# Turning q before its feature map, finer Sinkhorn tasks, and a second engine for one scaling: a change to a fused linear-attention and Sinkhorn mixture-of-experts kernel

## The chip, the cores and the metric

One core of one Trainium2 chip. The metric is the time of one execution on the device, in microseconds (us); lower is better. "Faster" and "slower" mean by over 2%. The profile's span is some 1.8 us shorter than the time of the same run.

The engines: TensorE (PE in the profile), VectorE (DVE), ScalarE (ACT), GpSimd (POOL). PSUM is the memory that TensorE writes; SBUF is the on-chip memory for everything else. "Turned" means transposed; a "cast" copies to another number format; an "eviction" copies a result out of PSUM, so that the PSUM bank can be filled again. kv, den, num and xt are TensorE's steps of attention, and kvz, qpT, rden, xn and xT are what the other engines make around them.

## The reference, cut to what matters

```python
def phi(x):                                   # feature map
    return np.where(x > 0, x, np.exp(x) - 1.0) + 1.0      # = max(x + 1, min(exp(x), 1))
q_p, k_p = phi(q), phi(k)                     # q, k, v: (8, 8, 576, 64) float32
kv = einsum('bhsd,bhse->bhde', k_p, v);  z = k_p.sum(axis=2)
x  = (q_p @ kv) / (q_p . z + 1e-6)            # -> x: (4608, 512)

P = exp(x @ w_gate - max)                     # (4608, 8)
for _ in range(8):                            # Sinkhorn: rows, then columns
    P /= P.sum(1) + 1e-9;  P /= P.sum(0) + 1e-9;  P *= N / E
for e in range(8):
    out += P[:, e:e+1] * (relu(x @ w1[e]) @ w2[e])
```

Attention is small; the eight experts are nearly all of TensorE's work. Expert 0 is computed beside attention, to fill TensorE's waits, and is scaled by its column of P once Sinkhorn is done.

## The kernel before

The kernel does not issue instructions in the order of its text. It describes tasks (engine or choice of engines, estimated us, dependencies, buffers), and a planner written in Python simulates them with these estimates and emits each engine's instruction list in the order in which the simulated tasks start. So an estimate changes the order of instructions and the choice of engine, not only a number in a table.

```python
class _Plan:
    def add(self, eng, fn, deps=(), prio=0.0, acq=(), use=(), lat=0.0, after=0.0): ...
    #  eng: ("dve", 0.49) or a choice {"dve": 0.6, "act": 1.17};  acq: takes a buffer of a pool
    def run(self):
        while left:
            ...                                   # the task that can start first, by prio
            t["start"] = te;  t["on"] = e;  t["done"] = te + t["eng"][e] + t["lat"]
            free[e] = te + max(0.0, t["eng"][e] - self.OVER.get(e, 0.0))
```

One attention block (two pairs of heads of one batch element; 16 blocks, n = 0 to 15). q and k take the same path: Exp on ScalarE, min and max on VectorE, all from SBUF. Then phi(q) is turned on TensorE, and copied out of PSUM:

```python
for nm in "kq":
    def f_e(_, ...):
        nc.scalar.activation(out=ge["tile"], in_=gin[nm]["tile"], func=AF.Exp)            # L266
    def f_t(e, ...):
        if e == "act":
            nc.scalar.add(out=..., in_=gin[nm]["tile"], add=1.0)                            # L272
    def f_m(_, ...):
        nc.vector.tensor_scalar(out=e, in0=e, scalar1=1.0, op0=ALU.min)                     # L275
        if g_["on"] == "act":
            nc.vector.tensor_tensor(out=o, in0=o, in1=e, op=ALU.max)                        # L278
        else:
            for r in range(2):
                nc.vector.scalar_tensor_tensor(out=o[:, r], in0=gin[nm]["tile"][:, r], scalar=1.0,
                                               in1=e[:, r], op0=ALU.add, op1=ALU.max)       # L281
... v is cast to float16 on GpSimd:  fadd(("pool", 1.3), f_v, ...)                          # L225
... kv_ps (banks ye2, ye3) <- tk, vv  (f_kv, L306);  kvz <- kv_ps
for j0, j1 in ((0, 5), (5, NJ)):
    gp = S_.grp(p_att)                                    # one of two "att" banks of PSUM
    def f_qt(...): nc.tensor.transpose(qt_ps, tq[:, j], ident)                              # L332
    def f_qc(e, ...): copy(e, qpT, qt_ps)                 # ScalarE or VectorE
... den (L347), rden, num (L371), xn = num * rden, xt (transpose, L387), xT <- xt
```

Expert 0: layer 1 writes `hq` in two PSUM banks (L536), its relu `h` is on ScalarE (L540), layer 2 writes `ye` (L706), then come its copy to `acc` and the scaling by P:

```python
def f_s(_, tt=tt, gg=gg):
    nc.vector.tensor_scalar(out=acc[g][:, tt, :], in0=acc[g][:, tt, :], scalar1=P_sb[:, gg, 0:1], op0=ALU.mult)
tf = add({"act": 0.59, "dve": 0.69}, f_fin, ...)
tf = add(("dve", 0.49), f_s, deps=[tf, p_done], prio=NG + g - 400.0)
```

The softmax here doesn't subtract the row's maximum and nothing guards it: scores larger than these inputs give would overflow.

Of the kernel before, what the change touches and what calls it, by code (L numbers as in the profile page):

```python
# [17 lines left out]
class _Plan:  # L18
# [13 lines left out]

    def add(self, eng, fn, deps=(), prio=0.0, acq=(), use=(), lat=0.0, after=0.0):

        if isinstance(eng, tuple):
            eng = {eng[0]: eng[1]}
        k = len(self.t)
        t = {"eng": eng, "fn": fn, "prio": prio, "acq": tuple(acq), "lat": lat, "kids": [], "nd": 0,
             "ready": after, "done": None, "id": k}
        self.t.append(t)  # L40
        for d in set(x for x in deps if x is not None):
            self.t[d]["kids"].append(k)
            t["nd"] += 1
        for g in list(acq) + list(use):
            g["users"].append(k)
        return k
# [5 lines left out]
    def run(self):  # L52
# [26 lines left out]
        while left:  # L79
# [25 lines left out]
            t["done"] = te + t["eng"][e] + t["lat"]  # L105
            free[e] = te + max(0.0, t["eng"][e] - self.OVER.get(e, 0.0))
            end = max(end, t["done"])
            for g in t["acq"]:
# [14 lines left out]
def kernel(  # L123
# [57 lines left out]
    p_in = {n: S_.pool(2) for n in "kvq"}  # L181
    p_e = S_.pool(2)
    p_t = {n: S_.pool(2) for n in "kq"}
# [8 lines left out]
    def load_w(ten, nm, pl, ap, cut, e, prio, parts=1, after=0.0, deps=()):  # L192
# [6 lines left out]
        for i in range(parts):  # L199
            def fn(_, i=i):  # L200
                dst, a, off = g["tile"], [list(x) for x in ap], e * DM * F
                if parts > 1:
                    n = a[cut][1] // parts
                    off += i * n * a[cut][0]
                    a[cut][1] = n
                    dst = dst[:, i * n:(i + 1) * n, :] if cut == 1 else dst[:, :, i * n:(i + 1) * n]
                nc.gpsimd.dma_start(out=dst, in_=AP(tensor=ten.tensor, offset=off, ap=a))
            ti = add(("pool", 1.0), fn, use=[g], prio=prio, deps=[tal])
            ts_.append(add(("dma", 6.0 / parts), lambda _: None, deps=[ti], use=[g], prio=prio, lat=2.6))
            w_last[0] = ti  # L210
# [15 lines left out]

    w_last, in_prev = [None], [None]
    front_ids = []
    xt_done = {}
# [7 lines left out]
    def att(b, g):  # L237
# [3 lines left out]
        def ps_home(i):  # L241
            if n < 2 and i < 2:
                return p_ye[i], yps, f"ye{i}"
            return p_att, aps, "att"

        src = [[NJ * D, P], [2 * S * D, 2], [1, NJ * D]]
        gin, tin, gt, tph = {}, {}, {}, {}
        for nm, ten in (("k", k), ("q", q), ("v", v)):
            gr = gin[nm] = S_.grp(p_in[nm])

            def fn(_, gr=gr, nm=nm, ten=ten):
                gr["tile"] = fp.tile([P, 2, NJ, D], FP32, tag=nm + "in", name=nm + "in", bufs=2)
                (nc.gpsimd if n in (2, 3) else nc.sync).dma_start(
                    out=gr["tile"].rearrange("p r j d -> p r (j d)"),
                    in_=AP(tensor=ten.tensor, offset=(b * H + 4 * g) * S * D, ap=src))
            ti = fadd(("pool", 1.0) if n in (2, 3) else ("sp", 0.45), fn, acq=[gr], prio=pr,
                      deps=[w_last[0] if n in (2, 3, 4) else None, in_prev[0]])
            in_prev[0] = ti
            tin[nm] = fadd(("dma", 1.55), lambda _: None, deps=[ti], use=[gr], prio=pr, lat=2.6)
        for nm in "kq":  # L260
            ge = S_.grp(p_e)
            gt[nm] = S_.grp(p_t[nm])

            def f_e(_, ge=ge, nm=nm):
                ge["tile"] = fp.tile([P, 2, NJ, D], FP16, tag="e", name="e" + nm)
                nc.scalar.activation(out=ge["tile"], in_=gin[nm]["tile"], func=AF.Exp)  # L266

            def f_t(e, g_=gt[nm], nm=nm):
                g_["tile"] = fp.tile([P, NJ, 2, D], FP16, tag="t" + nm, name="t" + nm)
                g_["on"] = e  # L270
                if e == "act":
                    nc.scalar.add(out=g_["tile"].rearrange("p j r d -> p r j d"), in_=gin[nm]["tile"], add=1.0)  # L272

            def f_m(_, ge=ge, g_=gt[nm], nm=nm):
                nc.vector.tensor_scalar(out=ge["tile"], in0=ge["tile"], scalar1=1.0, scalar2=None, op0=ALU.min)  # L275
                o = g_["tile"].rearrange("p j r d -> p r j d")
                if g_["on"] == "act":
                    nc.vector.tensor_tensor(out=o, in0=o, in1=ge["tile"], op=ALU.max)  # L278
                else:
                    for r in range(2):  # L280
                        nc.vector.scalar_tensor_tensor(out=o[:, r], in0=gin[nm]["tile"][:, r], scalar=1.0,  # L281
                                                       in1=ge["tile"][:, r], op0=ALU.add, op1=ALU.max)
            te = fadd(("act", 1.17), f_e, deps=[tin[nm]], acq=[ge], use=[gin[nm]], prio=pr)
            tt_ = fadd({"dve": 0.6, "act": 1.17}, f_t, deps=[tin[nm]],
                       acq=[gt[nm]], use=[gin[nm]], prio=pr)
            tph[nm] = fadd(("dve", 1.35), f_m, deps=[te, tt_], use=[ge, gt[nm], gin[nm]], prio=pr)
        gvv = S_.grp(p_vv)
# [5 lines left out]
        def f_v(e):  # L293
            copy(e, gvv["tile"][:, :, :, 0:D], gin["v"]["tile"])
        tvv.append(fadd(("pool", 1.3), f_v, deps=[ta, tin["v"]],
                        use=[gvv, gin["v"]], prio=pr))
        vcast[n] = tvv[0]
# [24 lines left out]
        def f_qa(_):  # L322
            gq["tile"] = fp.tile([P, 2, NJ, PW], FP16, tag="qpT", name="qpT")
        tqa = fadd(("none", 0.0), f_qa, deps=[tph["q"]], acq=[gq], prio=pr)
        tq = []
        for j0, j1 in ((0, 5), (5, NJ)):
            gp = S_.grp(p_att)

            def f_qt(_, j0=j0, j1=j1, gp=gp):
                gp["tile"] = aps.tile([P, 5, 2, PW], FP16, tag="att", name="qt_ps")  # L330
                for j in range(j0, j1):
                    nc.tensor.transpose(gp["tile"][:, j - j0, :, :].rearrange("p h w -> p (h w)"),  # L332
                                        gt["q"]["tile"][:, j, :, :].rearrange("p r d -> p (r d)"), ident)

            def f_qc(e, j0=j0, j1=j1, gp=gp):
                copy(e, gq["tile"][:, :, j0:j1, :].rearrange("p h j w -> p j h w"), gp["tile"][:, 0:j1 - j0])
            t1 = fadd(("pe", 0.06 * (j1 - j0)), f_qt, deps=[tph["q"], tqa], acq=[gp], use=[gt["q"]], prio=pr)
            tq.append(fadd({"act": 0.12 + 0.1 * (j1 - j0), "dve": 0.17 + 0.057 * (j1 - j0)}, f_qc, deps=[t1, tqa],
                           use=[gp, gq], prio=pr))
        js = [0, 2, 4, 6, 7]  # L340
# [74 lines left out]
    def sinkhorn():  # L415
# [9 lines left out]
        for it in range(8):  # L425
            def f_a(_, it=it):
                if it == 0:
                    nc.vector.tensor_reduce(ut, P0_sb, AXX.X, ALU.add)
                    nc.vector.tensor_scalar(out=Qr, in0=ut, scalar1=EPS, scalar2=None, op0=ALU.add)
                else:  # L430
                    nc.vector.tensor_tensor(out=wt, in0=P0_sb, in1=cc[:, None, :].broadcast_to([P, NTT, E]),
                                            op=ALU.mult)
                    nc.vector.tensor_reduce(ut, wt, AXX.X, ALU.add)
                    nc.vector.scalar_tensor_tensor(out=Qr, in0=Qr, scalar=EPS, in1=ut, op0=ALU.mult, op1=ALU.add)
                nc.vector.reciprocal(Rr, Qr)
                nc.vector.tensor_tensor(out=wt, in0=P0_sb, in1=Rr[:, :, None].broadcast_to([P, NTT, E]),
                                        op=ALU.mult)
                nc.vector.tensor_reduce(gs, wt.rearrange("p g e -> p e g"), AXX.X, ALU.add)
            gc = S_.grp(p_att)
# [5 lines left out]
            def f_d(_, it=it, gc=gc):  # L445
# [7 lines left out]
                nc.vector.reciprocal(cc, Dc)  # L453
            a = add(("dve", 2.85), f_a, deps=last, prio=-200.0)
            c = add(("pe", 0.2), f_c, deps=[a], acq=[gc], prio=-200.0, lat=0.15)
            last = [add(("dve", 0.65), f_d, deps=[c], use=[gc], prio=-200.0)]
# [238 lines left out]
    def unit_plain(e, g, gW=None, tW=None):  # L695
# [15 lines left out]
        for tt in range(4):  # L711
# [9 lines left out]

            def f_s(_, tt=tt, gg=gg):
                nc.vector.tensor_scalar(out=acc[g][:, tt, :], in0=acc[g][:, tt, :],
                                        scalar1=P_sb[:, gg, 0:1], scalar2=None, op0=ALU.mult)
            if e == 0:
                tf = add({"act": 0.59, "dve": 0.69}, f_fin, deps=[ty[tt], t_close if g >= NA else None],
                         use=[gy[tt]], prio=g - 400.0)
                tf = add(("dve", 0.49), f_s, deps=[tf, p_done], prio=NG + g - 400.0)
                for dh in range(2):
# [195 lines left out]
```

## Time and profile before

| | before |
|---|---|
| median, 3 runs | 982.81 us (982.53 to 983.16) |
| profiled run | 983.97 us, span 982.2 |
| TensorE busy | 962.2 us, 98% |
| TensorE idle before 125 us, 125 to 950 us, after | 14.1, 0.08, 5.8 us |

The profile's lines are in the prediction below. How to read them: a page line gives busy time and share of each engine; the 40 digits are the busy share of equal slices in tenths; a window row gives a stretch, then the busy us of PE, PEld, DVE, ACT and POOL, then clock and DMA; a gap line gives the start and length of a group of TensorE instructions, with the idle time before it and the instruction that ended it in brackets; a group line ends with count, total busy us, mean ns of one, and the idle time before it.

### The profile page before, as it was taken

How to read it: one execution, taken by the hardware profiler on the slowest of the kernel's cores; microseconds unless marked ns; L12 is line 12 of the kernel's file. 1: busy time of each engine (PE TensorE's matmuls, PEld its weight loads, DVE VectorE, ACT ScalarE, POOL GpSimd, SP SyncE). 2: the span in 40 equal slices, each digit the busy share in tenths (PEclk: the TensorE clock that was granted, in tenths of full speed). 3: DMA queues.
4: the chain of work that ended last, by engine and by line, in shares of the span. 5: the costliest groups of instructions: out<-in, count | busy, mean ns of one | idle time of the engine just before them, and what ended most of it. 6: DMA issues, size and time to landing. Idle time of an engine off the chain costs nothing.

```text
span 982.2 us, 21403 instructions
## 1 busy us (share of the span) xinstructions
PE 962.2 (98%) x8716; PEld 792.7 (81%) x8716; DVE 771.7 (79%) x1561; ACT 563.2 (57%) x1034; POOL 127.9 (13%) x171
## 2 busy tenths in 40 slices
PE   7899999999999999999999999999999999999997
PEld 4455564488888888888888888888888888888885
DVE  6898869967777777777777777777777777777774
ACT  4798754565555555555555555555555555555552
POOL 4111200001111111111111111111111111111110
PEclk9999999999999999999999999999999999999999
DMA  9886953162226312272225322272225322236663
GB/s 318 257 303 239 265 160 140 65 127 77 75 76 142 97 73 76 76 161 76 77 75 137 101 76 75 76 162 76 76 76 137 102 76 76 76 103 168 161 161 98
DMA packets 47029, 121.99 MB, mean 124 GB/s; under 512 B 4177, under 2 KB 18001, under 8 KB 46929
## 3 DMA queue, kind: packets, MB, share of 16 engines
q1 hardware_dynamic: 32128, 99.76, 30.3%
q0 software_dynamic: 14480, 20.33, 11.5%
q8 instruction: 68, 1.11, 0.5%
q10 hardware_dynamic: 320, 0.52, 0.1%
q14 instruction: 33, 0.26, 0.1%
HBM read 119.69 MB, written 17.69 MB: 140 GB/s over the span
## 4 chain that ended last, share of the span: by engine, by line
PE 89%; DVE 1%; ACT 1%; issue 0%
PE ye L809 33%; PE hq L627 23%; PE att L627 11%; PE Zye L627 6%; PE Zye L809 6%; PE ye L706 5%; PE hq L536 4%; PE xt_ps L387 0%; PE kv_ps L306 0%; PE num_ps L371 0%; PE lg_ps L405 0%; DVE tk L281 0%; PE qt_ps L332 0%; ACT tq L272 0%; PE den_ps L347 0%; ACT qpT L221 0%
## 5 line engine op out<-in xcount | busy, mean ns | idle before, releaser
L823 DVE SCALAR_TENSOR_TENSOR acc<-ye,P_sb,acc 128x256 f32<-128x256 f32 x620 | 264.9, 477 | 95.3 <-PE ye L809 77.9
L627 PEld LDWEIGHTS <-W 128*128 128x128 f16 x2016 | 197.1, 98 | 23.7
L809 PEld LDWEIGHTS <-S 128*128 128x128 f16 x1984 | 194.1, 98 | 22.7 <-issue 0.3
L809 PE MATMUL ye<-T,S 128*128 128x256 f16 x1488 | 192.8, 273 | 0.1
L833 POOL TENSOR_TENSOR acc<-acc,st 128x256 f32<-128x256 f32 x124 | 87.5, 725 | 625.6 <-ACT st L830 620.7
L653 ACT ACTIVATE h<-hq 128x512 f16<-128x512 f32 x126 | 76.3, 606 | 160.8 <-PE hq L627 160.8
L627 PEld LDWEIGHTS <-w 128*128 128x128 f16 x1512 | 147.6, 98 | 23.3 <-issue 1.0
L809 PEld LDWEIGHTS <-h 128*128 128x128 f16 x1488 | 145.6, 98 | 16.8
L627 PE MATMUL hq<-xs,W 128*128 128x256 f16 x1008 | 151.2, 273 | 0.0
L627 PE MATMUL att<-xs,W 128*128 128x256 f16 x1008 | 151.2, 272 | 0.0
L627 PE MATMUL hq<-xs,w 128*128 128x256 f16 x1008 | 140.7, 272 | 0.8 <-DVE h L656 0.8
L782 DVE TENSOR_TENSOR S<-h 128x1024 f16<-128x1024 f16 x124 | 85.4, 688 | 57.9 <-ACT h L653 57.9
L656 DVE CUSTOM_DVE_ANT_0 h<-att,s 128x512 f16<-128x512 f32 x126 | 86.7, 688 | 13.1 <-ACT s L643 13.1
L830 ACT ACTIVATE st<-Zye,P_sb 128x256 f32<-128x256 f32 x124 | 52.1, 471 | 78.0 <-PE Zye L809 78.0
L643 ACT COPY s<-hq 128x512 f32<-128x512 f32 x126 | 75.0, 595 | 36.7 <-PE hq L627 36.7
L650 ACT ACTIVATE h<-Zye 128x512 f16<-128x512 f32 x126 | 75.2, 597 | 35.1 <-PE Zye L627 35.1
L656 DVE CUSTOM_DVE_ANT_0 h<-hq,s 128x512 f16<-128x512 f32 x126 | 86.5, 686 | 0.8 <-PE hq L627 0.7
L639 ACT COPY Zye<-hq 128x512 f32<-128x512 f32 x126 | 73.3, 581 | 16.3 <-PE hq L627 16.3
L706 PE MATMUL ye<-w,h 128*128 128x512 f16 x320 | 77.6, 379 | 0.9 <-DVE acc L223 0.9
L627 PE MATMUL Zye<-xs,w 128*128 128x256 f16 x504 | 75.6, 273 | 0.0
L647 ACT COPY s<-att 128x512 f32<-128x512 f32 x126 | 74.5, 591 | 0.0
L536 PE MATMUL hq<-xT,w 128*128 128x512 f16 x288 | 70.6, 379 | 2.4 <-ACT h L540 2.2
(90 smaller groups left out, 963.1 us busy)
## 6 DMA issues: line engine op xcount, KB each, us to landing
xs<-xd SPq DMA_DIRECT2D x63, 896.0 KB, 4.6
w<-in_moe_w_dram POOLq DMA_DIRECT2D x14, 1024.0 KB, 11.7
out_dram<-acc SPq DMA_DIRECT2D x68, 128.0 KB, 2.4
kin<-in_k_dram SPq DMA_DIRECT2D x14, 576.0 KB, 6.0
qin<-in_q_dram SPq DMA_DIRECT2D x14, 576.0 KB, 5.0
vin<-in_v_dram SPq DMA_DIRECT2D x14, 576.0 KB, 6.4
xd<-xst SPq DMA_DIRECT2D x9, 512.0 KB, 2.6
xd<-xT SPq DMA_DIRECT2D x9, 256.0 KB, 7.1
```

The source lines that it names most:

```text
L536: nc.tensor.matmul(ghq["tile"], lhsT=gw1["tile"][:, c, ts(f, P)], rhs=xT[:, c, ds(512 * g, 512)], start=(c == 0), stop=(c == NDT - 1))
L627: nc.tensor.matmul(dst[:, p, :], lhsT=lhs(p, c), rhs=rhs(c), start=(first and p == 0 and c == 0), stop=(c == 1), skip_group_check=True)
L643: nc.scalar.copy(out=gs2["tile"], in_=gX["tile"])
L647: nc.scalar.copy(out=gs5["tile"], in_=gR["tile"])
L650: nc.scalar.activation(out=hd(0, 0), in_=Zt[1], func=AF.Relu)
L653: nc.scalar.activation(out=hd(1, 0), in_=gX["tile"], func=AF.Relu)
L656: nc.vector._custom_dve(TENSOR_ADD_SAT, out=dst, in0=ps, in1=sb, s0=3.0e38, s1=0.0)
L706: nc.tensor.matmul(gy[tt]["tile"], lhsT=gh["tile"][:, f, ds(P * tt, P)], rhs=gw2["tile"][:, f, :], start=(f == 0), stop=(f == NFT - 1))
L782: nc.vector.tensor_tensor(out=Sx[:, i], in0=a0, in1=a1, op=op)
L809: nc.tensor.matmul(bank(g_)[:, s, :], lhsT=lhs(s, kk), rhs=rhs(kk), start=(new and s == 0 and kk == 0), stop=(kk == 3), skip_group_check=True)
L823: nc.vector.scalar_tensor_tensor(out=dst(), in0=bank(g_)[:, s, :], scalar=P_sb[:, gg, e:e + 1], in1=dst(), op0=ALU.mult, op1=ALU.add)
L833: nc.gpsimd.tensor_tensor(out=dst(), in0=dst(), in1=gst["tile"], op=ALU.add)
```

## The change

The intent: take q's feature map off SBUF. Raw q is cast to float16 by GpSimd (which is busy for 30 of the first 125 us), turned on TensorE as it is, and phi is computed from PSUM, where the two-input step does the work of the old copy. Second, each step of Sinkhorn becomes its own task, so that other work can go between. Third, the planner may put the scaling of expert 0 by P on ScalarE as well. It also gets new estimates for GpSimd's tasks, and a "stall": a GpSimd cast holds VectorE back for 0.35 us in the simulation (0.9 us in the first two blocks).

```diff
+            if t["stall"]:
+                free["dve"] = max(free["dve"], te) + t["stall"]
...
+        def qt_home(half):
+            if n in QT_ATT:                       # QT_ATT = (1,)
+                return p_att, aps, "att"
+            return p_ye[2 + half], yps, f"ye{2 + half}"      # the banks of kv_ps
...
-        for nm in "kq":   (f_e, f_t, f_m as above)
+        def f_q(e):
+            copy(e, gt["q"]["tile"]..., gin["q"]["tile"])
+        tqq = fadd(QE[n] if n < 2 else ("pool", 1.2), f_q, ..., stall=QS[n] if n < 2 else 0.35)
+        (f_e, f_t, f_m for k alone)
...
-        tvv.append(fadd(("pool", 1.3), f_v, ...))
+        tvv.append(fadd(("pool", 1.2), f_v, ..., stall=... 0.35))
...
-            def f_qc(e, ...): copy(e, qpT, qt_ps)
+            def f_qe(_, ...):
+                nc.scalar.activation(out=eq, in_=qt_ps, func=AF.Exp)
+            def f_qm(_, ...):
+                nc.vector.tensor_scalar(out=eq, in0=eq, scalar1=1.0, op0=ALU.min)
+                nc.vector.scalar_tensor_tensor(out=qpT, in0=qt_ps, scalar=1.0, in1=eq, op0=ALU.add, op1=ALU.max)
...   (Sinkhorn: f_a, one task of 2.85 us, becomes a list of single instructions)
+            for us, op in seq:
+                last = [add(("dve", us), lambda _, op=op: op(), deps=last, prio=-200.0, lat=0.1)]
...
-            def f_s(_, tt=tt, gg=gg):
+            def f_s(eng, tt=tt, gg=gg):
+                if eng == "act":
+                    nc.scalar.mul(out=acc[g][:, tt, :], in_=acc[g][:, tt, :], mul=P_sb[:, gg, 0:1])
+                    return
...
-                tf = add(("dve", 0.49), f_s, deps=[tf, p_done], ...)
+                tf = add({"dve": 0.49, "act": 0.6}, f_s, deps=[tf, p_done], ...)
```

## The prediction

> **What bounds the kernel now.** I read the page first, then the table of stretches, then TensorE's gaps in order of time, then the groups of the first 205 us by shape. The page says which engine is full, and when:
>
> ```profile
> PE 962.2 (98%) x8716; PEld 792.7 (81%) x8716; DVE 771.7 (79%) x1561; ACT 563.2 (57%) x1034; POOL 127.9 (13%) x171
> ...
> PE   7899999999999999999999999999999999999997
> ```
>
> TensorE (PE) is busy 98% of the span, and only the first two slices and the last are below nine tenths. The table of stretches puts numbers to it (stretch, length, then busy us of PE, PEld, DVE, ACT, POOL, then clock and DMA):
>
> ```profile
> 0.00:125.00 125.00, 110.90 (x1154) 66.10 (x1154) 105.31 (x222) 94.91 (x150) 30.14 (x35) 0.99 0.89 276
> 125.00:205.00 80.00, 80.00 (x581) 43.85 (x580) 63.99 (x170) 42.47 (x77) 0.75 (x1) 1.00 0.38 118
> 205.00:950.00 745.00, 744.92 (x6782) 662.81 (x6780) 584.82 (x1138) 415.26 (x790) 94.17 (x131) 1.00 0.35 100
> 950.00:982.20 32.20, 26.36 (x207) 19.91 (x204) 17.56 (x34) 10.55 (x20) 2.83 (x4) 0.98 0.41 100
> ```
>
> From 125 us to 950 us TensorE has 0.08 us of idle. All it ever waits lies in the first 125 us (14.1 us) and at the end (5.8 us, which the change does not touch). "Busy" need not be "at peak", but the pace confirms it: in the chain of work that ended last, 16 matmuls of 512 columns take 3.47 us, 217 ns each, so work there is back to back. The change only touches attention, Sinkhorn and expert 0, that is, the first 205 us. Since both kernels have the same 17,410 rows on TensorE, its useful work is equal: **the time changes by the change in TensorE's idle time before about 125 us, and by little else.** Sinkhorn (140 to 180 us) and the scaling of expert 0 (181 to 202 us) lie where TensorE never waits.
>
> Within the 14.1 us, finer windows give 5.7 us of idle before 25 us, 4.1 from 25 to 50, 1.5, 1.6 and 1.2 in the three following quarters. TensorE's timeline names the gaps:
>
> ```profile
> 9.12 0.69 PE L306 MATMUL kv_ps<-vv,tk 64*128 64x130 f16 x18 [2.21 <-POOL vv L225]
> 10.90 0.68 PE L332 MATMUL qt_ps<-ident,tq 128*128 128x128 f16 x9 [1.09 <-DVE tq L281]
> ...
> 26.29 1.02 PE L536 MATMUL hq<-xT,w 128*128 128x512 f16 x4 [1.36 <-ACT h L540]
> ...
> 29.49 0.68 PE L332 MATMUL qt_ps<-ident,tq 128*128 128x128 f16 x9 [1.55 <-DVE tq L281]
> ...
> 44.63 1.02 PE L706 MATMUL ye<-w,h 128*128 128x512 f16 x4 [0.95 <-DVE acc L223]
> ```
>
> The brackets hold the idle time before a group and what ended it. Up to 9.1 us it is the arrival of the first inputs. Later gaps end with phi(q) on DVE (1.09, 1.55), with ACT's eviction of h (1.36), and with some ten small ones of 0.2 to 0.9 us, mostly DVE's (xn, qpT, acc). In addition 17 warm-up matmuls (yw) run after 9.1 us, some 5.7 us busy: they stand in for idle time of the start-up. The first real work of expert 0 starts at 22.53 us.
>
> **What the Trainium skill says.** (1) "SBUF — State Buffer", section "SBUF: two separate sides": GpSimd and VectorE share a port pair as an exclusive lock, taken by a DVE operation in a two-port mode or with two SBUF inputs, against a GpSimd operation; the loser blocks. The trace agrees: a pair of tk steps (L281, two SBUF inputs) takes 1.43 us at 6.60 us but 2.40 us at 12.41 us, when a cast of v starts on GpSimd at 12.39; the same again at 27.06 (2.37) and 76.36 (2.39). (2) "VectorE: DVE Perf Modes", section "Why PSUM operands drop a tier": a PSUM operand rules out the two-port modes. Here the two-input step xn from PSUM takes 0.68 us for 512 columns, one element a cycle plus some 0.15. (3) "ScalarE: Activation LUTs", "What ACT_TABLE_LOAD costs": one element a cycle for any function. Here Exp of 1152 takes 1166 ns, and a copy of 640 from PSUM 691 ns.
>
> **The change, part by part.** The groups that q leaves:
>
> ```profile
> L266 ACT ACTIVATE eq<-qin 128x1152 f16<-128x1152 f32 x16 | 18.7, 1166 | 0.3 <-DMA qin<-in_q_dram 0.3
> L281 DVE SCALAR_TENSOR_TENSOR tq<-qin,eq 128x576 f16<-128x576 f32 x16 | 12.4, 814 | 0.4
> ...
> L272 ACT ACTIVATE tq<-qin 128x1152 f16<-128x1152 f32 x8 | 9.4, 1169 | 0.0
> ...
> L275 DVE TENSOR_SCALAR eq<-eq 128x1152 f16<-128x1152 f16 x16 | 7.9, 496 | 0.6 <-ACT eq L266 0.6
> ...
> L278 DVE TENSOR_TENSOR tq<-tq,eq 128x1152 f16<-128x1152 f16 x8 | 6.1, 758 | 0.7
> ```
>
> With the copies of qpT (DVE 3.7 + 3.4, ACT 5.5 + 4.7) q costs DVE 12.4 + 7.9 + 6.1 + 7.1 = 33.5 us and ACT 18.7 + 9.4 + 10.2 = 38.3 us.
>
> - q, ACT: 16 Exp of 640 and 16 of 512 from PSUM at what copies of those sizes take (0.69 and 0.59) are 20.5 us, and one cast of q, 1.2. **21.7 in place of 38.3.**
> - q, DVE: for each of the 16, min over 640 and 512: a clean min of 1152 takes 0.45, which is 1152/3.84 = 300 ns plus 0.15 fixed, so 0.32 + 0.28. Then the two-input step from PSUM, 0.82 for 640 (640/0.96 + 0.15) and 0.68 for 512. Sum 2.10, times 16 = 33.6, and one cast of q on DVE, 0.75. **34.3 in place of 33.5: DVE gains nothing from q itself**, as the 1x step from PSUM eats what the copy and the old max cost.
> - GpSimd: 14 casts of q more, at the 1.24 us of v's: 17.4 us. With v's casts that is 30 in some 110 us; it is no bound.
> - The instruction order shows what the balance moves. kvz copies on DVE go from 30 to 12 (-3.9 us DVE, +3.8 ACT); phi(k) with its add on ACT from 5 to 8 of 16 (-3.2 DVE, +3.5 ACT); evictions of expert 0 on DVE from 6 to 12 (+4.1 DVE, -3.5 ACT); xT hardly.
> - Port clashes: the excess of DVE's k and q steps over their undisturbed length is (0.923 - 0.75)*22 + (0.814 - 0.75)*16 + 0.10*16 + 0.05*16 = 7.2 us for 16 casts. Casts double (30), but DVE's time with the shared port falls from 58 us to some 37, as the q step no longer reads two SBUF tensors: an estimate of 7.2*(30/16)*(37/58) = 8.6, so +1.4.
> - Sums: DVE +0.8 - 3.9 - 3.2 + 4.1 - 0.5 + 1.4 = -1.3 us, ACT -16.6 + 3.8 + 3.5 - 3.5 + 0.6 = -12.2 us, GpSimd +17.4. DVE stays at some 90% in the attention stage; ACT gets room.
> - Sinkhorn as single tasks: same instructions, finer order, in a stretch without TensorE idle: 0. Scaling by P: 13 of 36 go to ACT: 0.
>
> What TensorE sees. **Start-up**, walked by hand in the new order with these durations: the first q is cast on DVE only after phi(k) (8.0 to 8.75), turned by 9.3, Exp to 10.6, finished near 12.2; then ACT does k1's Exp and add and q1's cast (to 13.9) before the kvz copies, so the first den is near 16 us instead of 12.4. But the second half follows closely: both x are turned at about 22.4, and expert 0 starts at about 23, against 22.53: +0.4. **22 to 31 us**: the new order puts 8 layer-1 matmuls, the turning of q (long cast by GpSimd) and 12 more in a row; the waits that I find are for h, 0.5 + 0.3, against 0.2 + 1.4 + 1.6 before: -2.3. **31 to 125 us**: before, 5.3 us of gaps, each an eviction late by a fraction of a us. Freer ACT and a plan that knows the port stalls should take about half: -2.6 (this is judgement). Sum +0.4 - 2.3 - 2.6 = -4.5, so **978.3 us**.
>
> **Rivals.**
> (a) GpSimd's casts hold the port and arrive late; turned q then waits for GpSimd in place of DVE. For: each clash costs up to 1 us (2.40 against 1.43), casts double, and GpSimd runs in order, so a cast of v behind one of q waits for two loads. Against: GpSimd is idle four fifths of the stage and q is needed late. TensorE's gaps would stay: 982 to 985.
> (b) DVE's total does not fall, so DVE stays the limit of attention and gaps merely move: 980.5 to 983. For: the sums above, DVE at 105.3 of 125. Against: several gaps are ACT's or phi(q)'s, and TensorE has expert 0 to fill with.
> (c) Nearly all gaps after 25 us vanish (8.4 us) at an unchanged start-up: 974 to 975. More is not to be had, unless the start-up shortens.
>
> **Range and chances.** Rivals (c) and (b) set the ends: 974 to 983. Faster by over 2% would need 963, 19.7 us, more than all 14.1 us of early idle: 0.01. Slower by over 2%, 1002.5, would need TensorE's idle to more than double: 0.01.
>
> **What would show each step.** Right: idle of TensorE before 125 us falls from 14.1 to about 10, with the gap ended by tq on DVE gone; 125 to 950 still full; ACT's busy time in 0 to 205 about 12 us lower, DVE's about equal, GpSimd's up 17; expert 0 starting near 23 us; eq from PSUM near 0.69 and 0.59, the two-input step 0.82 and 0.68. Wrong: waits of TensorE for tq on GpSimd, tk steps above 0.92 us on the mean (rival a), or gaps of the same sum ended by qpT and xn (rival b); new idle after 125 us would break the main step.

## The result, and the profile after

| | before | after |
|---|---|---|
| median, 4 runs | 982.67 us (982.11 to 983.16) | 985.17 us (983.43 to 986.03) |
| ratio | | 1.0023 (95%: 1.0006 to 1.0041) |
| profiled run | 983.97 | 983.43 |

A ratio here is the mean time of one kernel's fast runs over the mean of the other's fast runs of the same rounds, so it is not quite the ratio of the medians. The change is within 2%, and 2.3 us slower by the means (984.95 against 982.65), where 4.5 us less had been predicted.

The page of the changed kernel, the lines that answer to those of before:

```profile
PE 964.9 (98%) x8716; PEld 793.0 (81%) x8716; DVE 767.9 (78%) x1541; ACT 559.6 (57%) x1056; POOL 143.8 (15%) x185
...
PE   8998999999999999999999999999999999999997
```

One slice, the fourth (74 to 98 us), now is below nine tenths. The table of stretches of the changed kernel:

```profile
0.00:125.00 125.00, 115.04 (x1226) 68.43 (x1227) 101.68 (x202) 88.75 (x167) 46.09 (x49) 0.99 0.83 264
125.00:205.00 80.00, 79.03 (x511) 42.09 (x509) 63.74 (x170) 45.95 (x83) 0.75 (x1) 1.00 0.48 136
205.00:950.00 745.00, 745.00 (x6784) 662.97 (x6783) 585.12 (x1139) 414.67 (x789) 94.56 (x132) 1.00 0.36 100
```

The idle time before 125 us did fall from 14.1 to 9.96 us, as predicted; but 0.97 us of idle is new after 125 us. TensorE's gaps, changed kernel:

```profile
9.06 0.68 PE L352 MATMUL qt_ps<-ident,tq 128*128 128x128 f16 x9 [1.97 <-DVE tq L225]
...
29.19 0.67 PE L324 MATMUL kv_ps<-vv,tk 64*128 64x130 f16 x17 [1.16 <-DVE qpT L362]
...
84.40 0.68 PE L324 MATMUL kv_ps<-vv,tk 64*128 64x130 f16 x17 [0.70 <-DVE qpT L362]
...
98.13 0.39 PE L399 MATMUL num_ps<-kvz,qpT 128*128 128x128 f16 x4 [1.25 <-DVE rden L381]
...
188.31 2.12 PE L564 MATMUL hq<-xT,w 128*128 128x512 f16 x8 [0.88 <-ACT h L568]
```

Two kinds are new. kv (L324) waits for phi(q) (qpT) of the block before: the turned q now lies in the banks that kv needs, which I had not read out of the diff. And at 188 us layer 1 waits for ScalarE, in the stretch that had no idle. No gap of 0.15 us or more between 24 and 205 us is ended by GpSimd. The groups of the first 130 us, changed kernel:

```profile
L362 DVE SCALAR_TENSOR_TENSOR qpT<-qt_ps,eq 128x640 f16<-128x640 f16 x16 | 13.2, 824 | 1.2
L357 ACT ACTIVATE eq<-qt_ps 128x640 f16<-128x640 f16 x16 | 11.3, 704 | 5.5 <-PE qt_ps L352 5.1
L227 POOL CAST tq<-qin 128x1152 f16<-128x1152 f32 x14 | 16.4, 1170 | 49.9 <-DMA qin<-in_q_dram 23.7 <-PE qt_ps L352 19.4 <-PE kv_ps L324 6.8
L300 DVE SCALAR_TENSOR_TENSOR tk<-kin,e 128x576 f16<-128x576 f32 x16 | 14.2, 927 | 0.3
L297 DVE TENSOR_TENSOR tk<-tk,e 128x1152 f16<-128x1152 f16 x8 | 9.4, 1179 | 0.8
```

The new operations cost what was predicted (0.82, 0.69, 1.2 us); the mean of k's tensor_tensor is 1179 ns, where q's in the trace of before took 758 and k's, in the second trace of before, 907.

**Why busy and idle time are not enough here.** By TensorE's idle time in these two traces, after should win by 3 us (10.9 against 14.2 before 950 us); the spans differ by 0.6, because 17 warm-up matmuls and the waits inside a group count as busy. So I worked out from each trace how much time TensorE had lost by a given moment: the moment, less the work issued by then at its undisturbed pace (216 ns for a matmul of 512 columns, 109 for 256, and 34, 56, 59 and 27 for those of kv, the transposes, num and den), with the warm-ups not counted as work. The same work is in every kernel, so the last column differs as the span does, within 0.2 us. The labels e1 to e14 are those of the experiments below. Us lost by the time at the head of the column:

```text
                               22.5   30   50   75  100  125  175  200 |  end    span
before (profiled run 983.97)   17.4 21.0 23.2 25.2 28.0 30.1 30.0 30.0 | 37.3   982.2
before again, e5               17.4 20.1 21.2 24.1 26.3 27.8 27.8 27.8 | 34.9   979.7
after  (profiled run 983.43)   17.4 19.3 20.7 22.1 26.4 28.1 28.4 29.8 | 36.8   981.6
after again, e1                17.8 19.3 20.7 21.6 26.1 29.0 29.2 30.9 | 37.7   982.6
e9  q's casts a sliver         17.4 18.6 20.2 22.1 24.1 26.7 26.7 28.3 | 35.3   980.1
e11 scaling on VectorE         17.2 19.1 20.6 21.4 25.2 27.9 28.6 28.6 | 35.4   980.2
e13 both                       17.2 18.4 19.8 20.9 23.3 25.8 26.3 26.3 | 33.3   978.2
e12 before + scaling on ACT    17.2 20.1 21.4 24.1 26.3 27.9 27.8 29.6 | 37.6   982.6
e6  before + idle casts        17.2 21.7 24.2 32.4 35.9 39.5 39.7 39.7 | 47.0   991.8
```

Read it along the rows of after and e5. By 75 us the change is ahead by 2.0 us. From 75 to 125 us it loses 6.0 where before loses 3.7, and the lead is gone. From 175 to 200 it loses 1.4 where before loses nothing. And the first row shows that the trace that the prediction rests on had lost 2.3 us more by 125 us than the second trace of the same kernel.

### The profile page after: what moved, and what is told of

The parts are those of the page before. It is cut to its first block, busy times and chain, and to the rows that moved or that the text cites. A ratio compares the mean times of both kernels' runs of the same rounds, so it can differ in the third digit from the quotient of the medians.

```text
span 981.6 us, 21435 instructions
## 1 busy us (share of the span) xinstructions
PE 964.9 (98%) x8716; PEld 793.0 (81%) x8716; DVE 767.9 (78%) x1541; ACT 559.6 (57%) x1056; POOL 143.8 (15%) x185
## 2 busy tenths in 40 slices
DMA packets 47027, 121.98 MB, mean 124 GB/s; under 512 B 4176, under 2 KB 18000, under 8 KB 46928
## 4 chain that ended last, share of the span: by engine, by line
PE 89%; DVE 5%; ACT 3%; DMA 2%; issue 1%; SPq 0%; DVEq 0%; ACTq 0%
PE ye L840 33%; PE hq L655 23%; PE att L655 11%; PE Zye L655 6%; PE Zye L840 6%; PE ye L734 4%; PE hq L564 4%; DVE qpT L362 1%; DMA kin<-in_k_dram 1%; DVE tk L300 1%; PE kv_ps L324 1%; DVE eq L361 1%; DMA xd<-xT 1%; PE xt_ps L415 0%; PE num_ps L399 0%
## 5 line engine op out<-in xcount | busy, mean ns | idle before, releaser
L840 PEld LDWEIGHTS <-S 128*128 128x128 f16 x1984 | 194.1, 98 | 22.5
L667 ACT COPY Zye<-hq 128x512 f32<-128x512 f32 x126 | 73.2, 581 | 17.4 <-PE hq L655 17.4
```

Source lines behind the costliest of these rows:

```text
L840: nc.tensor.matmul(bank(g_)[:, s, :], lhsT=lhs(s, kk), rhs=rhs(kk), start=(new and s == 0 and kk == 0), stop=(kk == 3), skip_group_check=True)
```

## The experiments

The theory after the result: (T1) the doubled casts on GpSimd block VectorE's two-input steps on k, and where that falls on TensorE's path it costs what the shorter q path gains. (T2) The scaling by P on ScalarE stands in front of expert 0's relu and costs 1 to 2 us at 190 us. The rivals: (R1) it is the shared banks, kv waiting for phi(q); (R2) it is the planner's new estimates, that is, another order; (R3) it is Sinkhorn's finer tasks. In the edits below, "kernel before" and "changed kernel" are whole kernels with only that edit.

### Changed kernel again, and kernel before again

> The changed kernel, unchanged, for its spread and for a second trace: the profiled run of the first measurement (983.4 us) was the fastest of four, the other three were 984.8 to 986.0. If the spread is of the kernel itself, it lies again between 983 and 986.5, ratio to before 1.001 to 1.004, and a second trace shows idle time of TensorE before 125 us that differs from the 9.96 us of the first by a microsecond or more. If the first traces can be trusted to 0.3 us, the new trace shows the same gaps of the same lengths.

Measured (e1): 984.59 (984.33 to 986.07), 1.0035 (1.0022 to 1.0047). The loss is real. Both of its traces have the same gaps of 0.70 and 1.25 us at 84 and 98 us, ended by qpT and rden.

> The kernel before, unchanged, for a second trace. The trace that the prediction rests on is of a run of 983.97 us, slower than all of the timed runs of that kernel so far (980.6 to 983.6). If that trace overstated the idle time (theory 3: a part of the gain that I predicted was only that run's bad luck), this one shows TensorE's idle time before 125 us at 11 to 13 us in place of 14.1, and the first matmul of expert 1's second layer near 206.5 us in place of 208.55. Otherwise they agree to 0.5 us.

Measured (e5): 982.04 (981.51 to 982.42), 0.9997 (0.9985 to 1.0008). Its trace has a span of 979.7 where the first one had 982.2. Its gap before the turned q, TensorE's timeline of before again:

```profile
28.52 0.68 PE L332 MATMUL qt_ps<-ident,tq 128*128 128x128 f16 x9 [0.61 <-DVE tq L281]
```

In the trace that I predicted from, this gap was 1.55 us, and I had counted it as something to win.

### Scaling back on VectorE, and the tail of before

```diff
-                tf = add({"dve": 0.49, "act": 0.6}, f_s, deps=[tf, p_done], ...)
+                tf = add(("dve", 0.49), f_s, deps=[tf, p_done], ...)
```

> The changed kernel with the scaling by P of expert 0 on DVE alone, as before; TensorE's and GpSimd's order stay word for word the same. Theory 1 (scalings placed on ACT stand in front of evictions of h in its queue; trace of the change: TensorE waits 0.88 us for h at 188.3, and five scalings of 0.6 run ahead of it): the gap at 188 goes, and the time falls by 0.9 to 2.5 us. Rival (all of the loss lies in the attention stage): no change beyond 0.4 us.

Measured (e2): 984.69 (983.05 to 985.35), 1.0028 (1.0015 to 1.0040). The gap at 188 us is gone (0.1 us lost between 175 and 200), but this trace had lost 1.2 us more than e1's by 125 us, under the same order of instructions on TensorE. By the means it is only 0.7 us better than e1: not clear of the spread.

> The changed kernel with Sinkhorn in blocks and the scaling on DVE, as both were before; so only the new q path, its PSUM homes and the new cost figures are left. If Sinkhorn's single tasks matter not (my prediction), this is within 0.4 us of the run with the scaling alone undone. If they delay P and by that the scaling and evictions (theory 1b), it is faster than that run by over 0.5 us. Its distance to the kernel before is what the new q path itself is worth: my prediction said -4.5 us; the rival that gaps only moved says -1 to +2.

In addition Sinkhorn's steps as one task per round again. Measured (e3): 984.36 (983.16 to 985.76), 1.0027 (1.0015 to 1.0040), against 1.0028 without that edit: R3 falls; the finer tasks do nothing measurable, as predicted.

> The second run of the changed kernel with the scaling on DVE alone, to settle its size: both traces of the change show 1.4 and 1.7 us lost between 175 and 200 us, behind scalings in ScalarE's queue, but the first timed runs without it were faster by only 0.7 us on the mean. If the gap is what it costs, this lies 1.2 to 1.8 us below the changed kernel (983.2 to 983.8) and its trace loses under 0.3 us there; otherwise within 0.5 us of 985.0.

Measured (e11): 983.15 (982.00 to 984.33), 1.0012 (1.0000 to 1.0025). The three kernels without the scaling on ScalarE (e2, e3, e11; 15 runs) have a mean of 984.0, the changed kernel (9 runs) 985.0. So it costs some 1.0 us across calls, with the calls from 0.7 to 1.9.

### The scaling alone, on the kernel before

```diff
 (kernel before)
+                if eng == "act":
+                    nc.scalar.mul(out=acc[g][:, tt, :], in_=acc[g][:, tt, :], mul=P_sb[:, gg, 0:1])
+                    return
-                tf = add(("dve", 0.49), f_s, deps=[tf, p_done], ...)
+                tf = add({"dve": 0.49, "act": 0.6}, f_s, deps=[tf, p_done], ...)
```

> The kernel before with that one part of the change alone: scaling by P of expert 0 on ScalarE or VectorE as the plan chooses. The first 180 us are those of before. If scalings in front of evictions in ScalarE's queue cost TensorE time, this is 0.7 to 2 us slower than before, with a wait of TensorE for h or acc near 185 to 190 us; if the loss seen in the change has to do with its later P only, within 0.4 us.

Measured (e12): 984.64 (984.42 to 987.03), 1.0033 (1.0019 to 1.0046): this part alone makes the kernel before slower by 3.0 us by the means, of which its trace shows 1.8 between 175 and 200 us. ScalarE's timeline of this run:

```profile
184.39 1.34 ACT L724 ACTIVATE acc<-acc,P_sb 128x512 f32<-128x512 f32 x2
185.61 0.59 ACT L221 COPY acc<-ye 128x512 f32<-128x512 f32 x1
186.08 2.58 ACT L724 ACTIVATE acc<-acc,P_sb 128x512 f32<-128x512 f32 x4
188.54 0.60 ACT L540 ACTIVATE h<-hq 128x512 f16<-128x512 f32 x1
```

and TensorE's:

```profile
189.19 1.02 PE L536 MATMUL hq<-xT,w 128*128 128x512 f16 x4 [1.42 <-ACT h L540]
```

Layer 1 ends 8 matmuls at 187.77, two filled banks, and can go on only when ScalarE has emptied one. Six scalings and a copy stand in front of that relu in ScalarE's list, and the trace shows them run first. The scalings become ready together, when Sinkhorn's last step is done. T2 holds.

### q's turned tiles in the other banks

```diff
-    QT_ATT, QT_HQ = (1,), ()
+    QT_ATT, QT_HQ = tuple(range(16)), ()
```

> The changed kernel with the turned q in the att banks for all 16 blocks, as before the change, in place of the two banks of the kv products. Theory 2 (sharing a single-buffered bank with kv makes kv of the next block wait for phi of q: TensorE's waits of kv for qpT were 2.2 us and kv's busy time grew by 1.8 us): those waits go and the time falls by 1 to 4 us. Rival (the att banks are the scarcer ones: q now holds them for Exp, min and max, about 2.5 us a half, in place of a copy of 0.6): the time rises by 1 to 5 us, with den and num waiting instead.

Measured (e4): 998.54 (997.21 to 998.78), 1.0167 (1.0153 to 1.0181). R1 falls, at least as a remedy: the waits of kv for qpT (four, 2.2 us in all, in the changed kernel) are gone, and den, num and xt wait instead for a bank of "att". The same waits also shrink while the banks stay shared: to 0.9 us with q's casts cut short (the sliver below, e9), and to 0.2 with v's cut as well (e10). So the shared banks alone don't make them. TensorE's timeline, this run (e4):

```profile
93.02 0.41 PE L375 MATMUL den_ps<-kvz,qpT 128*128 128x2 f16 x10 [1.06 <-DVE qpT L362]
...
103.44 0.42 PE L375 MATMUL den_ps<-kvz,qpT 128*128 128x2 f16 x10 [1.41 <-ACT e L284]
```

With the turned q now held through Exp, min and max instead of one copy, it keeps its bank longer. The change's own choice of banks is worth 13 us.

### Casts that nobody reads, on the kernel before

```diff
 (kernel before, blocks n >= 2)
+            def f_xc_(_):
+                xq = fp.tile([P, NJ, 2, D], FP16, tag="xq", bufs=1)
+                nc.gpsimd.tensor_copy(out=xq..., in_=gin["q"]["tile"])
+            fadd(("pool", 1.2), f_xc_, deps=[tin["q"]], use=[gin["q"]], prio=pr)
```

> The kernel before with 14 more casts of q on GpSimd, into a tile that nobody reads; the order on TensorE, VectorE and ScalarE is word for word that of before. Theory 4 (GpSimd's casts hold the port that it shares with VectorE, which delays phi(k) and phi(q) and so TensorE): the time rises by 1.5 to 5 us, and the mean of the two-input steps tk and tq by 0.05 us or more each. Rival (the casts lie beside other work, as the prediction took them: +1.4 us of VectorE time, hidden): within 0.8 us of before.

Measured (e6): 993.27 (992.39 to 993.57), 1.0109 (1.0096 to 1.0123). TensorE, ScalarE and VectorE have the same instructions in the same order as in the kernel before; GpSimd has 14 more casts, with no reader. They cost 10.8 us by the means. The q step of VectorE, before again:

```profile
L281 DVE SCALAR_TENSOR_TENSOR tq<-qin,eq 128x576 f16<-128x576 f32 x16 | 12.2, 806 | 0.4
```

and with the casts:

```profile
L281 DVE SCALAR_TENSOR_TENSOR tq<-qin,eq 128x576 f16<-128x576 f32 x16 | 21.0, 1352 | 0.4
```

So a cast on an idle engine is not free here. One cast costs TensorE 0.77 us on the mean (10.8/14), for this order. In this order casts fall on q's own two-input step, which in the changed kernel reads PSUM, so the 0.77 us can't be carried over to the changed kernel.

### q's cast not on GpSimd

```diff
-fadd(QE[n] if n < 2 else ("pool", 1.2), f_q, ..., stall=QS[n] if n < 2 else 0.35)
+fadd(QE[n] if n < 2 else {"dve": 0.75, "act": 1.17}, f_q, ...)
```

> The changed kernel with q's cast on VectorE or ScalarE (the plan chooses: 11 and 5 of 16) in place of GpSimd. Theory 4 (port clashes are what cost the gain): the single-source cast takes 0.75 us on VectorE, less than the clashes of a GpSimd cast, so the time falls by 1 to 3 us. Rival (VectorE's own time is the limit of the stage): +8 us of VectorE time make it 2 to 6 us slower.

Measured (e7): 985.51 (985.06 to 987.68), 1.0036 (1.0024 to 1.0048): no gain. 11 of the 16 casts went to ScalarE and 5 to VectorE, so VectorE got five casts of 0.75 us and not the 8 us that the expectation counts. This doesn't clear GpSimd: the casts' time on the other two engines takes the place of the clashes, and the planner's order is another one (in this trace TensorE waits 1.4 us for weights at 33 and 39 us, which it does nowhere in the changed kernel's). The run changes three things at once and settles nothing; the sliver below changes only one.

### Old estimates in the planner

```diff
-("pool", 1.2), ..., stall=0.35)     -("pool", 0.85)   -("pool", 0.78)
+("pool", 1.3), ...)                 +("pool", 1.0)    +("pool", 1.0)
```

> The changed kernel planned with the old cost figures: GpSimd's DMA issues at 1.0, casts at 1.3, no stall of VectorE behind a GpSimd cast. Only the order changes. If the new figures do the plan good, this is 0.5 to 4 us slower; if they are without effect, within 0.7 us; if they make it too cautious, faster.

Measured (e8): 988.43 (985.91 to 990.74, 6 runs), 1.0055 (1.0042 to 1.0068). R2 falls, as far as these estimates go: without them the same work is some 3 us slower still. Its profiled run was its slowest (990.74), so I read no gap out of it.

### q's casts cut to a sliver

```diff
-            copy(e, tq..., gin["q"]["tile"])
+            w = 2 if e == "pool" else D                 # 2 of 64 columns; the rest stays at zero
+            copy(e, tq[:, :, :, 0:w]..., gin["q"]["tile"][:, :, :, 0:w])
```

> The changed kernel with GpSimd's cast of q cut to 2 of 64 columns (from the third block on; the result is wrong on purpose, the rest of the tile is a constant); the order on TensorE, VectorE and ScalarE is that of the changed kernel but for two memsets at the start. It takes the long GpSimd casts away and leaves everything else. In the traces of the change TensorE's lost time grows by 6 to 7.4 us between 75 and 125 us, against 3.7 to 4.9 in the kernel before. Theory 4 (clashes with those casts give back the gain): that growth falls to 3 or 4 us and the time by 2 to 5 us, to 980 to 983, at or below the kernel before. Rival (the longer chain through the shared banks, transposition, Exp, min, max, next kv, gives it back): less than 1 us of change, the gaps of kv behind qpT stay.

Measured (e9): 982.25 (980.38 to 982.58), 0.9998 (0.9985 to 1.0010). The planner's estimates are untouched, so TensorE, ScalarE and VectorE get the same instructions in the same order as in the changed kernel (but for two memsets at the start); only the length of 14 casts differs, 267 ns on the mean in place of 1170. That gives 3.2 us by the means (981.8 against 985.0, across calls; 0.25 to 0.37% by the ratios). (The values are not meant to be right; the difference stays within the tolerance.) VectorE's timeline around the largest gap, the changed kernel:

```profile
95.62 2.37 DVE L300 SCALAR_TENSOR_TENSOR tk<-kin,e 128x576 f16<-128x576 f32 x2
97.92 0.17 DVE L381 TENSOR_SCALAR rden<-den_ps 128x20 f32<-128x20 f32 x1
98.11 0.28 DVE L383 RECIPROCAL rden<-rden 128x20 f32<-128x20 f32 x1
```

GpSimd's timeline there, the changed kernel:

```profile
95.92 1.46 POOL L227 CAST tq<-qin 128x1152 f16<-128x1152 f32 x1 [3.17 <-PE qt_ps L352]
```

and VectorE's with the sliver:

```profile
93.92 1.45 DVE L302 SCALAR_TENSOR_TENSOR tk<-kin,e 128x576 f16<-128x576 f32 x2
95.29 0.17 DVE L383 TENSOR_SCALAR rden<-den_ps 128x20 f32<-128x20 f32 x1
95.49 0.28 DVE L385 RECIPROCAL rden<-rden 128x20 f32<-128x20 f32 x1
```

The pair of k steps takes 2.37 us beside the cast and 1.45 without it. rden stands right behind it on VectorE, and TensorE's num waits for the bank that rden's first step reads: the wait is 1.25 us there and 0.32 in this run, on TensorE's timeline with the sliver:

```profile
95.50 0.39 PE L401 MATMUL num_ps<-kvz,qpT 128*128 128x128 f16 x4 [0.32 <-DVE rden L383]
```

T1 holds, and this is its mechanism at one place, from instruction to wait.

> The same with v's cast cut as well from the third block on (also wrong on purpose): no long GpSimd instruction is left in the attention stage. If clashes per cast cost about the same for q and v, this gains as much again as the run with q alone; if GpSimd's casts are not what costs, both are within 1 us of the changed kernel. What is left after it is the cost of the chain itself.

v's casts cut in the same way (wrong; the relative error is 1.06). Measured (e10): 981.13 (980.66 to 982.52), 0.9994 (0.9981 to 1.0006), 0.4 us below e9 by the means, where as much again as the first gain was expected, with 1.46 us of new waits for weights at 33 and 38 us in its trace. So taking away the clashes of v's casts too ended in another wait here.

To size the clashes I added up, for the first 130 us, what VectorE's instructions took over the shortest of their own form:

```text
before 11.3   before again (e5) 8.9   before + idle casts (e6) 19.8
after 14.1    after again (e1) 15.2   scaling on VectorE (e11) 15.4
q sliver (e9) 12.4   q sliver, scaling on VectorE (e13) 10.5   q and v sliver (e10) 6.2     us
```

Not all of it is clashes (e10 keeps 6.2). The change adds 3 to 6 us of it, and the sliver takes only 2 to 5 away (e9 against after and e1, e13 against e11); most of the rest goes with v's casts, as e10 has 6.2. Of what remains in e9, little falls where TensorE waits: its excess from 75 to 100 us is 0.24 us, counting cases over 0.15, against 2.93 in the changed kernel. The sum alone doesn't tell the cost; the place does.

Which instructions are these? I paired each VectorE instruction that is over 0.15 us above its shortest, up to 130 us, with what GpSimd does at that time. In the changed kernel there are 15, nine of them steps of min and six of k's steps with two inputs; 14 run beside a cast (4.5 us beside q's casts, 6.0 beside v's), and the last beside a transfer that GpSimd is issuing. In the kernel before all 8 run beside v's casts (7.2 us). With the sliver none is beside q's casts and 8.4 us are beside v's: a part of the clashes has only moved, and the mean of the k steps is the same as in the changed kernel (929 ns and 927).

### Both causes taken away, and a correct version without the cast

> The changed kernel with both suspects off at once: the GpSimd casts of q cut to 2 of 64 columns (values not meant to be right) and the scaling of expert 0 by P back on VectorE. Alone, the first gave 0.9998 of the kernel before and the second 1.0012 to 1.0028, against 1.0023 and 1.0035 for the changed kernel. If the casts cost some 3 us and the scaling on ScalarE some 1.5 us, and the two are separate, this gives 980.2 to 980.8 where the kernel before gives 982 (0.9982 to 0.9990). If one hides the other it stays at 0.9995 or above.

Measured (e13): 979.97 (978.17 to 980.77), 0.9976 (0.9963 to 0.9990). TensorE, ScalarE and GpSimd have the order of the kernel with the scaling on VectorE (e11). The two effects add: 0.9976 against 0.9998 with the sliver alone and 1.0012 with the scaling alone. This is the one run that is clearly ahead of the kernel before, by 2.3 us. It is not a version to use, as its q is not computed.

```diff
 (scaling on VectorE; blocks n >= 2: no float32 q, no cast)
+                for r in range(2):
+                    nc.gpsimd.dma_start(out=tq[:, :, r, :], in_=AP(tensor=q.tensor, ..., ap=[[NJ * D, P], [D, NJ], [1, D]]))
```

> A correct version without the casts: from block 2 on, q is loaded as float16 by transfers of GpSimd's queue (two each, 128 bytes a run), so that no engine converts it; scaling by P on VectorE. If only the cast's hold on VectorE matters and the transfers arrive in time, as for the sliver: 980 to 981.5 (0.998 to 0.9995). If the small runs make q late or GpSimd's issuing (an estimated 1.6 us in place of a cast of 1.17) holds VectorE or v's cast back, the gain is lost: 983 to 987, with TensorE's waits for tq now ended by a transfer.

Measured (e14): 988.42 (986.56 to 989.19), 1.0063 (1.0050 to 1.0076), and correct. The transfers of this run (kilobytes each, median us from issue to landing):

```profile
kin<-in_k_dram SPq DMA_DIRECT2D x14, 576.0 KB, 4.4
...
tq<-in_q_dram POOLq DMA_DIRECT2D x28, 144.0 KB, 8.6
```

A quarter of the bytes takes twice the time, and on another queue: the converting transfer writes runs of 128 bytes, and packets under 512 bytes rise from 4,176 to 36,656. The Trainium skill, "DMA: Bandwidth & Descriptors", section "Specifications", gives 512 bytes as the least for full rate. The run fits this, but it changes the queue and adds the conversion as well, so it doesn't show which of the three costs the time. GpSimd is also busy 28.1 us issuing the 28 (1007 ns each), more than the 16.4 of the casts. The expected wait of TensorE for these transfers did not show: none of its gaps ends with one. By the account above 0.9 us of the loss is the start-up (18.1 us by 22.5, where VectorE's one cast of q took 1714 ns in place of 754) and the rest is spread to 125 us (33.6 against e11's 27.9). VectorE's sum of excess, as above, is 9.0 us here against 15.4 in e11, so the clashes did shrink; but six of its steps of min, 1.8 us in all, are late with no cast beside them, each while GpSimd is issuing a transfer. How the rest of the loss comes about, beside a granted clock of 0.93 from 50 to 75 us in this trace, stays open; e14 is 5.0 us over e11 by the means (988.2 and 983.2).

## Why the prediction was wrong, step by step

**Right.** TensorE's useful work is equal and 205 to 950 us stays full (745.00 of 745). The start-up: first layer-1 work of expert 0 at 22.55 us, lost time 17.4 in both, against +0.4 predicted. The durations of Exp and of the two-input step from PSUM; the steps of min took 0.41 and 0.35 us where 0.32 and 0.28 were worked out, and 0.31 and 0.29 without the long casts (e10). The layer-1 wait for h at 26 us and the wait for tq at 29 us are gone. GpSimd's busy time rose 15.9 us (17.4 predicted). Sinkhorn's finer tasks: nothing (e3). Rival (c)'s end of the range was never near.

**Wrong: "Port clashes ... so +1.4", put only into VectorE's sum.** I took the clashes as a part of VectorE's load, found that the load fell by 1.3 us in all, and so gave them no time of their own on TensorE's path. Their size was off (3 to 6 us more excess, where +1.4 was worked out; the sum counted tk, tq and their min, but not k's tensor_tensor, whose mean rose from 759 to 1179 ns, 3.4 us in all). But the failed step is to count clashes in a sum of load at all: the clash of 0.92 us in front of rden was 0.93 us of TensorE's wait (1.25 against 0.32), whatever VectorE's share of the stage was. Runs e9 and e13 put q's casts at 3.2 and 3.4 us of the time. This is rival (a)'s first half, which I gave 982 to 985 and left out of the range. Its second half, turned q waiting for GpSimd, did not happen, and the other sign that I named for it could not show it: the mean of the tk steps is 923 ns in the trace of before, 927 in the changed kernel and 929 with the sliver, which gains 3.2 us.

**Wrong: "31 to 125 us ... freer ACT and a plan that knows the port stalls should take about half: -2.6".** In that stretch the lost time went from 7.7 us (e5, 30 to 125 us) to 8.8. Even without the casts' length (e13) it is 7.4. The freer ScalarE did come: from 31 to 125 us its busy time fell from 78.8 us (79.6 in e5) to 71.2, and VectorE's from 83.4 (82.4) to 78.7. So what failed is the step from more room on these engines to half the gaps. (Over the whole span ScalarE fell by only 3.6 us, 563.2 to 559.6, where -12.2 was worked out: the scalings, 13 of 718 ns or 9.3 us, were left out of its sum.)

**Wrong: "Scaling by P: 13 of 36 go to ACT: 0".** The reason given was that TensorE never waits there. No idle is not the same as slack: in before's trace ScalarE idles only some 0.3 us between two relus of expert 0 in a row, and layer 1 has two banks, so a run of four scalings (2.58 us) cannot be hidden. I looked at TensorE's idle time there and not at ScalarE's timeline, where two lines of before show it:

```profile
182.28 0.60 ACT L540 ACTIVATE h<-hq 128x512 f16<-128x512 f32 x1 [0.33 <-PE hq L536]
...
188.28 0.60 ACT L540 ACTIVATE h<-hq 128x512 f16<-128x512 f32 x1 [0.28 <-PE hq L536]
```

The bracket is all that ScalarE had to spare before each. The runs put the cost at 0.7 to 1.9 us in the changed kernel, some 2 us beside the sliver (e9 to e13), and 3.0 on the kernel before.

**Wrong in size: "22 to 31 us ... -2.3".** Most of what was to be won was bad luck of one run. From 22.5 to 30 us the trace used lost 3.6 us, the second trace of before 2.7, the changed kernel 1.9. The gain against a usual run is 0.8.

**The account.** Without both costs the change is worth -2.3 us (e13), half of the -4.5 predicted. q's casts on GpSimd give back some 3.2, the scaling on ScalarE 1 to 2: +1.9 to +2.9 in sum, against +2.3 and +3.3 measured (means against means). What is not settled: why the same kernel varies by 1.5 us either way. The two traces of before, with one order, differ in VectorE's excess (11.3 and 8.9) as in lost time (30.1 and 27.8 by 125 us), which speaks for clashes that fall differently with the arrival of transfers, but no run varied that alone. That the clashes alone, and not also GpSimd's shorter occupation, make the sliver's gain is likewise only argued: no gap ends with GpSimd, but v's casts do come earlier, and their clashes move with them.

## What to carry to other kernels

Work moved to an idle engine is free only if that engine shares nothing with a busy one: look for each new instruction's neighbour on the shared port, and count the clash where it falls, on the path, not in the engine's sum. A stretch without idle may have no slack either: ask how far ahead the engine runs that empties its buffers before putting tasks without a waiter into that engine's list. And for an effect of less than 2 us, take two traces of the kernel before: a wait that is in only one of them can't be won.

## What the Trainium skill lacked or had wrong

- "SBUF — State Buffer", section "SBUF: two separate sides", names the lock and who blocks, and the traces agree; it has no word on what a clash costs a kernel that another engine bounds. Here a blocked pair of two-input steps takes 2.37 us in place of 1.45, and 14 casts cost the time 10.8 us in one order of instructions (e6) and some 3.2 us in another (e9).
- "DMA: Bandwidth & Descriptors" has the 512-byte rule, but no time for a converting load that breaks it: here 144 KB in runs of 128 bytes landed after 8.6 us from GpSimd's queue, beside 4.4 us for 576 KB of plain load from SyncE's, and issuing one took GpSimd 1007 ns.
- No page that I read says how far two traces of one kernel differ: here 2.5 us of span (982.2 and 979.7), all of it in the first 130 us or so.
